# Pooled attention and an affine residual MLP on one core: the first mix freed of later row sums, batch 1's q over TensorE, and batch 1's attention placed later

## The chip, the cores and the metric

The kernel runs on one core of a Trainium2 chip. The metric is device time in microseconds (us), the median of several executions. Before the change it is 346.08 us (three runs, 345.53 to 347.93). The profile shown here is of one execution whose instructions span 343.4 us.

The engines are called TensorE (PE in the profile, with its weight loads as PEld), VectorE (DVE), ScalarE (ACT), GpSimd (POOL) and the sync engine (SP), which only issues transfers. "POOLq" and "SPq" are the instruction queues of GpSimd and the sync engine as issuers of transfers.

## The reference

There are 8 batches, 8 heads, 576 rows and a head width of 64, so a row over all heads is 512 wide. k and v are averaged over groups of 8 rows, which leaves 72 keys per head. Then follows a token mix over the 576 rows and a channel MLP of width 2048.

```python
k_p = k.reshape(B, H, Sp, pool, D).mean(axis=3)
v_p = v.reshape(B, H, Sp, pool, D).mean(axis=3)
scores = scale * np.matmul(q, k_p.transpose(0, 1, 3, 2))
attn = softmax(scores)                       # max subtracted, sum + 1e-9
x = heads_joined(np.matmul(attn, v_p))       # (B, 576, 512)

a1 = alpha1 * x + beta1
tok = np.einsum('ts,bsd->btd', w_tok, a1)
u = x + lam * tok
a2 = alpha2 * u + beta2
ch = np.maximum(a2 @ w_ch1, 0.0) @ w_ch2
out = u + lam * ch
```

## The kernel before

**Chunks and blocks.** The output rows are cut into chunks of 128 rows: four chunks `(b, 0)` to `(b, 3)` for each batch, and one chunk `(b, 4)` for each pair of batches that holds the last 64 rows of both. Four chunks make a block of the MLP, so there are nine blocks. Block 0 holds batch 0's four chunks, block 1 batch 1's four chunks.

**The MLP of a block.** `mlp_A(n, j)` (L641) computes one of 16 tiles of the hidden layer: four matmuls of 512 columns into `ps_h`, then a Relu on ScalarE into `Hj` (L658). `mlp_B(n, m, part)` (L663) computes a quarter of one output chunk: four matmuls of 512 columns into `ps_ch`. After part 3 VectorE multiplies by lam and adds u (L693, L694), and the sync engine stores the chunk.

**The attention of a batch.** It runs one batch ahead of its block: while TensorE works on block n, the attention of batch n + 1 is threaded in.

- `att_F` (L383) transposes q, either on TensorE with a ScalarE copy (L397, L404) or with a transposing transfer on the sync queue (L392). `att_K` (L432) pools k on TensorE after GpSimd has summed it (`sum_k`, L179). `att_S4` (L501) computes the scores of four heads, with the exponentials on ScalarE (L541); batch 0 uses `att_S` (L485) head by head.
- `sum_v` (L129) and `first_V` (L459) pool v for batch 1; later batches use `att_V` on VectorE (L476). Batch 1's v comes over `load_v32` (L117), on the GpSimd queue.
- `att_AV` (L545) multiplies the weights of one head with v: five matmuls of 66 columns (L556, L560), then a reciprocal and a product on VectorE (L562, L564) that write the head into `x_tm`. `att_X` (L574) makes `xs`, two heads at a time, on VectorE or GpSimd (L578, L571).

**Token mix.** `mix_T(b, c)` (L603) multiplies the transposed w_tok with all of `xs` of a batch: five matmuls of 512 columns into `ps_tok`. It therefore needs all eight heads of the batch. VectorE adds x (L614) and makes `u_bf` (L617), and `mix_uT` (L619) transposes that into `u_fm`, the MLP's input: in block 0 on TensorE with a copy on ScalarE (L631, L633), later with a transposing transfer on the sync queue (L626).

**Setup.** `setup_wtok(t)` (L318) transposes a block of w_tok on TensorE, and ScalarE copies it into `wtT`. `setup_rowsum(t)` (L331) computes the row sums of that block, which go into one more row of `wtT` and carry the beta term; `mix_T(0, c)` reads the row sums of block c. `setup_vectors` (L311) turns beta2 into columns. `keep_warm` (L597) issues matmuls whose result nobody reads. `load_w1(g)` and `load_w2(g)` (L357, L363) fetch parts of the two channel weights over the GpSimd queue; `load_w1(2)` is the last quarter of w_ch1.

**What sets the order.** The kernel schedules by hand. Up to block 0's first tiles the calls stand in the source in the order in which each engine gets them (L703 to L787). After that, each block makes a list `todo` of pairs of a position and a call (L841 to L877), sorted by position and issued in that order; one unit of position is one `mlp_A` tile or one `mlp_B` quarter. `mlp_A` of tile j stands at j, and `mlp_B` at 16 and later. Every engine runs its own instructions in that order, so a position ties an instruction only to its neighbours on its engine. Batch 1 has positions of its own (`first`), and the loads of batch 2 stand behind small memsets on VectorE (`gate`, `behind`) that hold them back.

The softmax here doesn't subtract the row's maximum and nothing guards it: scores larger than these inputs give would overflow.

## Time and profile before

| What | Value |
|---|---|
| Time, median of 3 runs | 346.08 us (345.53 to 347.93) |
| Span of the profiled execution | 343.4 us |
| First `mlp_A` of block 0 starts | 27.40 us |
| First mix of batch 1 starts | 54.44 us |
| First `mlp_A` of block 1 starts | 68.69 us |
| HBM read / written | 38.30 MB / 9.44 MB |
| Share of the chain of waits on TensorE | 83% |

The page gives for each engine its busy time, its share of the span and its number of instructions; then the span in 40 slices, each digit the busy share in tenths. `PEclk` is the clock that TensorE was granted, in the same tenths. A table of stretches lists, for each stretch of the span, the length and then the busy time of PE, PEld, DVE, ACT and POOL with instruction counts, then the clock, the DMA share and the rate in GB/s. A timeline line gives the start and the length in us, the engine, the line of the kernel, what is written and read with the shapes, and a count; in square brackets stands how long the engine was idle before it and what ended that. Neighbouring matmuls of one line are merged, and the length of a merged line reaches over into the next, since matmuls are pipelined; starts are the better guide.

### The profile page before, as it was taken

To read this page: it belongs to the slowest core of one execution; us is meant where nothing else is said; L and a number is where in the kernel's file an instruction comes from. 1 tells how busy PE (TensorE), PEld (TensorE's weight loads), DVE (VectorE), ACT (ScalarE), POOL (GpSimd) and SP (SyncE) were. 2 spreads that over 40 slices of the span, in tenths; PEclk is the share of its full clock that TensorE was granted. 3 is DMA by queue.
4 is the path that set the end of the run, shared out by engine and by line. 5 is a ranking of instruction groups with operands and counts; after the bars stand their busy time and mean duration, and the time that the engine had idled before them with its cause. 6 is when DMAs were issued, how large, how long until landed. Compare 5 with 4: busy or idle time off the path is not lost.

```text
span 343.4 us, 5828 instructions
## 1 busy us (share of the span) xinstructions
PE 333.8 (97%) x2162; PEld 176.4 (51%) x2198; DVE 222.1 (65%) x478; ACT 145.9 (42%) x275; POOL 91.1 (27%) x106
## 2 busy tenths in 40 slices
PE   7998999999999999999999999999999999999995
PEld 2767654455445544455445544554455445545544
DVE  6774388985777677866866697768675881037511
ACT  3756870069106820385038500880089006604700
POOL 8869507301153012701170218002600200000000
PEclk9999999999999999999999999999999999999999
DMA  8999999758688906794599439972910132011012
GB/s 119 201 212 329 200 210 275 156 139 140 159 231 162 176 1 175 165 226 58 159 173 208 67 111 216 170 125 67 239 42 1 48 76 76 2 61 62 2 51 71
DMA packets 67086, 46.03 MB, mean 134 GB/s; under 512 B 35401, under 2 KB 57293, under 8 KB 67058
## 3 DMA queue, kind: packets, MB, share of 16 engines
q1 hardware_dynamic: 52772, 32.99, 40.5%
q0 software_dynamic: 13824, 12.40, 21.7%
q8 instruction: 17, 0.28, 0.4%
q10 hardware_dynamic: 462, 0.27, 0.3%
q14 instruction: 11, 0.09, 0.1%
HBM read 38.30 MB, written 9.44 MB: 139 GB/s over the span
## 4 chain that ended last, share of the span: by engine, by line
PE 83%; DMA 9%; DVE 3%; POOL 1%; issue 1%; SPq 0%; ACT 0%; DVEq 0%; POOLq 0%
PE ps_ch L687 32%; PE ps_h L652 32%; PE ps_tok L610 11%; DMA w<-in_moe_w_ch_dram 4%; DMA rem_raw<-in_k_dram 2%; PE ps_av L556 2%; PE ps_s L512 2%; DMA q_bf<-in_q_dram 2%; DMA u_fm<-u_bf 1%; PE ps_ch L676 1%; DVE x_tm L564 1%; PE ps_kp L440 1%; PE ps_sc L492 1%; PE ps_r L519 1%; POOL k_raw L183 0%
## 5 line engine op out<-in xcount | busy, mean ns | idle before, releaser
L658 ACT ACTIVATE Hj<-ps_h,bias_cols 128x512 bf16<-128x512 f32 x144 | 97.9, 687 | 166.4 <-PE ps_h L652 163.9
L652 PE MATMUL ps_h<-u_fm,w 128*128 128x512 bf16 (+2 forms) x575 | 132.2, 374 | 2.1 <-ACT u_fm L633 0.7
L687 PE MATMUL ps_ch<-w,Hj 128*128 128x512 bf16 x543 | 128.5, 379 | 0.9 <-issue 0.5
L652 PEld LDWEIGHTS <-w 128*128 128x128 bf16 x592 | 64.1, 114 | 53.1 <-issue 3.9
L687 PEld LDWEIGHTS <-Hj 128*128 128x128 bf16 x560 | 52.9, 98 | 61.7 <-issue 1.6
L610 PE MATMUL ps_tok<-xs,wtT 128*128 128x512 bf16 (+2 forms) x199 | 44.7, 380 | 0.7 <-DVE xs L578 0.3
L693 DVE TENSOR_TENSOR ps_ch<-lam_bc,ps_ch 128x512 f32<-128x512 f32 x32 | 22.2, 693 | 34.0 <-PE ps_ch L687 33.8
L578 POOL TENSOR_TENSOR xs<-x_tm,lamal_bc 128x512 bf16<-128x512 f32 x10 | 12.6, 1268 | 110.2 <-DVE x_tm L564 110.2
L614 DVE TENSOR_TENSOR u_sb<-x_tm,ps_tok 128x512 f32<-128x512 f32 (+1 forms) x40 | 27.4, 684 | 11.9 <-PE ps_tok L610 11.9
L564 DVE TENSOR_TENSOR x_tm<-ps_av,rec 128x320 f32<-128x320 f32 x64 | 31.5, 492 | 2.7
L562 DVE RECIPROCAL rec<-ps_av 128x5 f32<-128x5 f32 x64 | 12.3, 193 | 31.7 <-PE ps_av L560 31.6
L694 DVE TENSOR_TENSOR u_sb<-u_sb,ps_ch 128x512 f32<-128x512 f32 x35 | 24.0, 687 | 13.6 <-PE ps_ch L687 12.5
L541 ACT ACTIVATE ET<-ps_s 72x512 f16<-72x512 f32 x56 | 32.3, 591 | 0.0
L610 PEld LDWEIGHTS <-wtT 128*128 128x128 bf16 (+3 forms) x200 | 17.4, 100 | 21.6 <-issue 2.5
L617 DVE TENSOR_TENSOR u_bf<-u_sb,al_bc 128x512 bf16<-128x512 f32 x34 | 25.6, 754 | 2.6 <-DMA u_fm<-u_bf 1.5
L480 DVE TENSOR_TENSOR v_u<-v_u 72x512 f32<-72x512 f32 (+1 forms) x48 | 26.4, 550 | 0.8
L183 POOL TENSOR_TENSOR k_raw<-k_raw 128x512 f32<-128x512 f32 x14 | 19.7, 1404 | 10.7 <-DMA k_raw<-in_k_dram 10.7
L556 PEld LDWEIGHTS <-ET 72*128 72x128 f16 x256 | 14.0, 97 | 9.1 <-DVE vp L473 0.4
L185 POOL TENSOR_TENSOR k_bf<-k_raw 128x512 bf16<-128x512 f32 x14 | 17.8, 1271 | 1.1
L79 POOL DMA_DIRECT2D q_bf<-in_q_dram x16 | 12.5, 784 | 15.3 <-DVE v_u L158 14.5
L578 DVE TENSOR_TENSOR xs<-x_tm,lamal_bc 128x512 bf16<-128x512 f32 x22 | 15.5, 705 | 0.7
L556 PE MATMUL ps_av<-vp,ET 72*128 72x66 f16 x256 | 15.6, 193 | 0.1
(130 smaller groups left out, 214.4 us busy)
## 6 DMA issues: line engine op xcount, KB each, us to landing
out_dram<-u_sb SPq DMA_DIRECT2D x32, 256.0 KB
k_raw<-in_k_dram SPq DMA_DIRECT2D x12, 512.0 KB
v_u<-in_v_dram SPq DMA_DIRECT2D x12, 512.0 KB
q_bf<-in_q_dram POOLq DMA_DIRECT2D x16, 256.0 KB, 6.2
w<-in_moe_w_ch_dram POOLq DMA_DIRECT2D x6, 512.0 KB, 15.3
w<-in_moe_w_ch_dram POOLq DMA_DIRECT2D x1, 1024.0 KB, 14.6
k_raw<-in_k_dram POOLq DMA_DIRECT2D x2, 512.0 KB, 16.8
v_main<-in_v_dram POOLq DMA_DIRECT2D x1, 1024.0 KB, 11.8
```

The source lines that it names most:

```text
L480: nc.vector.tensor_tensor(out=t[:, :, 0:n], in0=t[:, :, 0:n], in1=t[:, :, n:2 * n], op=ALU.add)
L541: nc.scalar.activation(out=o, in_=i, func=AF.Exp, bias=0.0, scale=0.125)
L556: nc.tensor.matmul(out=av[:, odd + c, :], lhsT=ET[:, m0:m0 + 128], rhs=vp1[:, hh, :])
L564: nc.vector.tensor_tensor(out=x[:, 1 - odd:6 - odd, dd:dd + D], in0=av[:, :, 0:64], in1=rec.unsqueeze(2).to_broadcast((P, 5, D)), op=ALU.mult)
L578: eng.tensor_tensor(out=xs[:, 0:4, cols], in0=x[:, 1:5, cols], in1=lamal_bc[:, cols].unsqueeze(1).to_broadcast((P, 4, D * (h1 - h0))), op= ...
L610: nc.tensor.matmul(out=ps_tok[p0:p1], lhsT=wtT[0:kk, at, P * c:P * c + p1 - p0], rhs=xs_pool[i][0:kk, sc, :], start=(sc == 0), stop=(sc == 4))
L614: nc.vector.tensor_tensor(out=s["u"][p0:p1, :], in0=x[p0:p1, 1 + c if c < 4 else 5 - 5 * i, :], in1=ps_tok[p0:p1, 0:DM], op=ALU.add)
L617: eng.tensor_tensor(out=s["u_bf"], in0=s["u"], in1=al2_bc, op=ALU.mult)
L652: nc.tensor.matmul(out=ps_h[:, t0:t1 + one], lhsT=w1_of(cc, j), rhs=rhs, start=(cc == 0), stop=(cc == 3))
L658: nc.scalar.activation(out=t, in_=ps_h, func=AF.Relu, bias=bias_cols[:, j:j + 1], scale=1.0)
L687: nc.tensor.matmul(out=ps, lhsT=Hj[n, j][:, 128 * m:128 * m + 128], rhs=w2[j // 4][:, j % 4, :], start=(j == 0), stop=(j == NJ - 1))
L694: nc.vector.tensor_tensor(out=u, in0=u, in1=ps, op=ALU.add)
```

## The change

Four things are changed; the computation is the same.

1. **Order of the prologue.** Head 4's `att_AV` moves ahead of head 6's scores. The w_tok transposes start earlier, and `mix_T(0, 0)` comes right after the row sums of block 1 instead of after those of block 2 and the fourth w_tok transpose. `setup_vectors` moves behind `mix_T(0, 1)`, with its second copy on ScalarE instead of VectorE. `mix_T(0, 3)` comes after the first two `mix_uT` instead of between them. There is one `keep_warm` matmul less. The aim is that the first mix waits only for what it reads.
2. **q of batch 1.** Its second half too is transposed on TensorE, at positions 2.6, 3.5, 4.4 and 5.3, instead of by a transposing transfer.
3. **Loads.** `load_w1(2)` is issued ahead of `load_v32(1)` instead of behind it.
4. **Batch 1's attention.** The row sums of v, `first_V` and the eight `att_AV` are placed later and closer together, the mixes start at 22.6 with a spacing of 1.2 instead of at 21.0 with 1.3, and the gated loads of batch 2 move from 14.5 to 17.5. This follows from the later v.

```diff
     def setup_vectors():
         ...
-        nc.vector.tensor_copy(out=u_fm[0][:, :, 0, 256], in_=ps[:, 0:4])
+        nc.scalar.copy(out=u_fm[0][:, :, 0, 256], in_=ps[:, 0:4])
...
-        if b > 1 or b == 1 and u:
+        if b > 1:
             if r == 0:
                 nc.sync.dma_start_transpose(out=st["qT"][u],
...
     att_S(0, 5)
+    att_AV(0, 4)
     att_S(0, 6)
-    att_AV(0, 4)
     spread_al1(1)
     att_AV(0, 5)
     att_X(0, 4, 6, nc.gpsimd, False)
     att_S(0, 7)
-    keep_warm(1)
+    setup_wtok(0, nc.scalar.copy)
     att_AV(0, 6)
-    setup_vectors()
     load_rem(1, behind=nc.vector)
     keep_warm(1)
-    setup_wtok(0, nc.scalar.copy)
+    setup_wtok(1, nc.scalar.copy)
+    keep_warm(1)
     att_AV(0, 7)
-    setup_wtok(1, nc.scalar.copy)
-    keep_warm(2)
+    keep_warm(1)
+    setup_rowsum(0)
     setup_wtok(2, nc.scalar.copy)
-    setup_rowsum(0)
     rest_X(0, 4, 6, nc.gpsimd)
     load_w1(1)
     keep_warm(1)
     setup_rowsum(1)
+    att_X(0, 6, 8)
+    mix_T(0, 0, nc.gpsimd)
     setup_rowsum(2)
     setup_wtok(3, nc.scalar.copy)
-    att_X(0, 6, 8)
-    mix_T(0, 0, nc.gpsimd)
-    load_v32(1)
+    load_w1(2)
     mix_T(0, 1)
+    setup_vectors()
     setup_rowsum(3)
     mix_T(0, 2, nc.gpsimd)
-    load_w1(2)
+    load_v32(1)
+    mix_uT((0, 0))
+    mix_uT((0, 1))
+    mix_T(0, 3)
     load_w2(0)
-    mix_uT((0, 0))
-    mix_T(0, 3)
-    mix_uT((0, 1))
     load_w2(1)
-    att_F(1, 2)
     mlp_A(0, 0, 0, 256)
...
         if first:
-            for hp in range(2):
-                todo.append((2.6 + 1.4 * hp, lambda hp=hp: att_F(b, hp)))
+            for hp in range(4):
+                todo.append((2.6 + 0.9 * hp, lambda hp=hp: att_F(b, hp)))
...
-            early = (5.7, 6.2, 4.2, 4.7) if first else (5.7, 6.2, 2.9, 3.4)
-            for i, dt in enumerate((2.9, 3.4, 4.6, 5.1) if u else early):
+            late = ((7.5, 8.1, 6.3, 6.9), (4.2, 4.8, 5.5, 6.1))[u]
+            for i, dt in enumerate(late if first else (2.9, 3.4, 4.6, 5.1) if u else (5.7, 6.2, 2.9, 3.4)):
                 h = 4 * u + i
                 todo.append((at + dt, lambda h=h: att_AV(b, h)))
...
             for i, u in enumerate((0, 2, 1)):
-                todo.append((10.4 + 0.1 * i, lambda u=u: sum_v(b, u)))
+                todo.append((12.7 + 0.1 * i, lambda u=u: sum_v(b, u)))
             for u in range(2):
-                todo.append((12.1 + 1.3 * u, lambda u=u: first_V(b, u)))
+                todo.append((14.6 + 0.9 * u, lambda u=u: first_V(b, u)))
...
         for c in range(5):
-            at = 21.0 + 1.3 * c
+            at = (22.6 + 1.2 * c) if first else 21.0 + 1.3 * c
...
-                    at = (14.51 if b == 1 else 21.0) + 0.01 * u
+                    at = (17.51 if b == 1 else 21.0) + 0.01 * u
                     todo.append((at, lambda b=b, u=u: load_k(b + 1, u, gate)))
...
-                    at = 14.55 + 0.01 * u if b == 1 else (6.7 if b == 2 else 3.5) + 4.0 * u
+                    at = 17.55 + 0.01 * u if b == 1 else (6.7 if b == 2 else 3.5) + 4.0 * u
                     todo.append((at, lambda b=b, u=u: load_v(
...
-                todo.append((14.5 if b == 1 else 20.9, lambda b=b: load_rem(b + 1, behind=gate)))
+                todo.append((17.5 if b == 1 else 20.9, lambda b=b: load_rem(b + 1, behind=gate)))
```

## The prediction

> **What bounds the kernel now.** I read four views, in this order: the page's busy rows and slices, the table of stretches, the timeline of each engine from 15 to 75 us, and the chain of waits in the same stretch.
>
> ```profile
> PE 333.8 (97%) x2162; PEld 176.4 (51%) x2198; DVE 222.1 (65%) x478; ACT 145.9 (42%) x275; POOL 91.1 (27%) x106
> PEclk9999999999999999999999999999999999999999
> 25.00:30.00 5.00, 4.09 (x38) 3.18 (x37) 3.16 (x9) 2.34 (x4) 4.98 (x8) 1.00 1.17 316
> 30.00:50.00 20.00, 19.94 (x204) 12.93 (x205) 9.76 (x31) 16.86 (x36) 8.58 (x9) 1.00 1.14 231
> 50.00:55.00 5.00, 4.69 (x36) 2.24 (x34) 4.51 (x12) 0.00 (x0) 2.46 (x3) 1.00 1.17 265
> 55.00:69.00 14.00, 13.90 (x69) 6.17 (x69) 12.29 (x18) 0.00 (x0) 6.28 (x6) 1.00 0.88 192
> ```
>
> After the stretch and its length come PE, weight loads, DVE, ACT, POOL, the clock, and DMA. TensorE is idle 343.4 - 333.8 = 9.6 us in all. Only two holes lie where the diff reaches: 0.91 us in 25 to 30 and 0.31 us in 50 to 55. From 30 to 50 TensorE has no hole to give back, and from batch 2 on the instruction orders of both kernels are the same. So the end moves by whatever the start of block 1 (68.69 us) moves.
>
> The two holes, and what runs into the second, in the timelines of TensorE and VectorE (start, length, instruction, count, idle before it):
>
> ```profile
> 27.40 0.60 PE L652 MATMUL ps_h<-u_fm,w 128*128 128x257 bf16 x4 [0.67 <-ACT u_fm L633]
> 30.00 1.93 PE L652 MATMUL ps_h<-u_fm,w 128*128 128x256 bf16 x16 [0.23 <-DVE bias_cols L655]
> 54.44 1.24 PE L610 MATMUL ps_tok<-xs,wtT 128*128 128x512 bf16 x5 [0.31 <-DVE xs L578]
> ...
> 44.89 0.20 DVE L562 RECIPROCAL rec<-ps_av 128x5 f32<-128x5 f32 x1 [0.53 <-PE ps_av L560]
> 51.61 0.18 DVE L562 RECIPROCAL rec<-ps_av 128x5 f32<-128x5 f32 x1
> 52.23 0.18 DVE L562 RECIPROCAL rec<-ps_av 128x5 f32<-128x5 f32 x1
> 53.60 0.69 DVE L578 TENSOR_TENSOR xs<-x_tm,lamal_bc 128x512 bf16<-128x512 f32 x1
> ```
>
> VectorE starts batch 1's eight heads at 44.89 us and works with only about 0.2 us of gaps until the last xs at 54.29, which starts mix_T(1,0) at 54.44. That run of VectorE work is the figure to carry along.
>
> Last, the sync queue ahead of block 1 (transposes of batch 1's u), and two u_bf products on VectorE:
>
> ```profile
> 64.84 1.19 SPq L416 DMA_TRANSPOSE rem_qT<-rem_q  x1
> 66.12 1.22 SPq L626 DMA_TRANSPOSE u_fm<-u_bf  x1
> 68.26 0.34 SPq L696 DMA_DIRECT2D out_dram<-u_sb  x1
> ...
> 59.10 1.31 DVE L617 TENSOR_TENSOR u_bf<-u_sb,al_bc 128x512 bf16<-128x512 f32 x1
> 64.07 0.69 DVE L617 TENSOR_TENSOR u_bf<-u_sb,al_bc 128x512 bf16<-128x512 f32 x1
> ```
>
> The last transpose that block 1 needs was issued at 66.12 and block 1 ran at 68.69: 2.57 us, with only 0.2 us of weight-load wait on it. So u_fm is already only just in time.
>
> **What the Trainium skill says.** "TensorE: Matmul & The Clock Gate", "Back-to-back issue gap": 518 cycles for 512 columns; the trace agrees, 0.86 us for four. Its "Part 1: The HAM clock gate" says the clock falls after an idle window of about 3.4 us; no hole in this trace is that long, the clock stays full in every slice, and my holes below stay under it. "SBUF — State Buffer", "SBUF: two separate sides": a VectorE operation with two SBUF inputs and a GpSimd operation that reads SBUF exclude each other. The trace agrees: L617 took 1.31 us at 59.10, while GpSimd summed k, against 0.69 us at 64.07.
>
> **Part by part.**
>
> *Prologue order.* The first mix now needs only rowsums 0 and 1 ahead of it; rowsum 2 and the fourth w_tok block follow. VectorE's last xs (19.92 to 20.9 us) is hardly moved: the removed bias copy (0.17 us) is offset by head 7's matmuls, which now stand behind one more w_tok transpose group. So mix_T(0,0) starts when that xs is there, at about 20.8 instead of 21.50. Behind it: rowsum 2 and w_tok 3 (0.28 each), mix 1 (1.08), the vector transpose (about 0.15), rowsum 3 (0.28), mix 2 (1.08), two groups of transposes (0.22 each), mix 3 (1.08). That puts the first mlp_A at 26.5 instead of 27.40, with its 0.67 us hole filled by mix 3. The next gate is u_bf of the fourth chunk (0.69 + 0.8 us on VectorE after mix 3), its transpose and ScalarE's 0.59 us copy: the second halves start at about 29.3 instead of 30.00. Gain 0.7 us; 0.55 if that gate binds fully, 0.88 if not. One filler matmul less (0.22) is inside this.
>
> *q over TensorE.* Eight more transposes (two groups of four, 0.22 us each by the group at 31.77): +0.44 us on the full engine. ScalarE's two more copies (0.59 each) lie in gaps of 0.3 to 0.7 us that it has from 30 to 48. The removed sync-queue transpose (27.61, 1.35 us) was awaited by nobody on the path.
>
> *Loads.* Before, v_main was issued at 24.78 and landed 11.8 us later (36.6); w_ch1's last quarter was issued at 27.55 and landed about 14.4 us later, at 42, just as setup_bias(3) wanted it (0.2 us of wait). Swapped, the weights come early and v last of the two, at about 42. Three row sums (0.67 + 0.42, 0.67, 0.67 + 0.42 = 2.85 us) then end at 45, against first_V(1,0) at 45.9: hidden, 1 to 2 us spare. w_ch2's third and fourth quarters landed about 15.7 and 15.0 us after 33.51 and 36.68; their issues move by about 0.4 us, and uses at about 51.9 and 53.6 leave over 1 us.
>
> *Batch 1's attention later.* Now the decisive sum. The first head goes from position 13.2 to 15.3, the last from 18.7 to 19.7, so eight heads are packed into 4.4 positions. Net of the prologue and the q transposes TensorE ends the first head's matmuls at about 47.1 us. From there to mix_T(1,0), now at 22.6 and behind part 3 of the first output chunk, it has first_V 0.22, seven heads at 0.15 and seven groups of four matmuls at 0.864: 7.3 us, so it arrives at 54.4. VectorE has, for the same stretch, eight heads at 0.63 (51.61 to 52.23), copies of vp 0.48, two xs pairs at 1.03 (0.69 + 0.29 and gaps), the gate memsets 0.5, the last xs 0.70, and about 0.4 for the longer first head and latencies: 9.1 us. It ends at about 56.3. TensorE waits about 2.0 us (1.5 to 2.3) where it waited 0.31: +1.7 us. One group of output matmuls has moved ahead of the wait, but it is in the 7.3 us and comes off later, so it changes nothing in the difference.
>
> *Start of block 1.* After mix_T(1,0) starts at 56.35, TensorE has 14.25 - 0.86 = 13.4 us (54.44 to 68.69 less that group): ready at 69.7. The transpose of the fourth chunk may not be: mix_T(1,3) is later (26.2), and its transpose (28.0) now stands on the sync queue behind the store of chunk m=2 (27), which waits for VectorE. VectorE's order after the last xs is m=0, u0, m=1, u1, u2, u3, m=2, each pair about 1.4 us: u_bf 3 ends at 65.6 to 66.2, m=2 at 67.0 to 67.6, store 0.35, transpose issued at 67.5 to 68.0, landing 2.57 us later at 70.0 to 70.6. That is 0.3 to 0.9 us of new wait; I take 0.5. The gates for batch 2's loads move from 48.05 to about 52.4; k and v then come some 4 us later, but k was ready at 62.9 for a use at 73.0, and v is next used at 70.2, moving to about 72: hidden.
>
> Sum: -0.7 + 0.44 + 1.7 + 0.5 = +1.9 us. 346.08 + 1.9 = 348.0.
>
> **Rivals.** (a) VectorE's run does not bind: the packed heads are drained while TensorE is in its seven groups, and only the prologue's gain and the extra transposes remain, with the 0.31 us hole closed: -0.7 + 0.44 - 0.31 = -0.6, 345.5; at best 345.2. For it: TensorE is the busy engine, and the attention is moved by about as much as the mixes (2.1 and 1.6 positions). Against: VectorE took 9.4 us for this work without real gaps, and 7.3 us is all it is given. (b) The wait at the first mix comes, but u_fm is in time: -0.7 + 0.44 + 1.7 = +1.4, 347.5. (c) A load joins in: v lands at 45 rather than 42, holding first_V, all heads and VectorE by some 2 us, or the sync queue holds u_fm behind v loads of batch 2 by 2 to 3 us. Then +4 to +5, 350 to 351. For it: v is read from a queue whose transfers took 11.8 to 17.9 us; against: bytes and order ahead of it are those that ended at 42.
>
> **How the numbers follow.** Waits at both places, +1.6 to +2.6 us: 50 in 100. (b): 23. (a), wholly or in part: 17, nearly all of it within 1% of before. (c): 10. The likeliest gives 348.0. The range leaves out most of (c) and the tail of (a): 345.5 to 349.4. Over 1% slower means 349.5 or more: (c) and a little of the first, 0.11. Over 1% faster would need 3.5 us, and the holes in reach sum to 1.2: 0.02. The rest, 0.87, is within 1%.
>
> **What would show it.** In the changed profile: mix_T(0,0) at 20.8 and the first mlp_A at 26.5 without the 0.67 us hole; sixteen q transposes between 31 and 36 us; mix_T(1,0) with about 2 us of idle laid to VectorE's xs, near 56.3; block 1 at about 70.2 with a wait on u_fm; later blocks 36 us apart as before. Wrong if mix_T(1,0) starts without a wait, if the row sums of v wait for their load past 43 us, or if the clock leaves full speed.

## The result: 350.05 us, slower by about 1%

| | Before | After |
|---|---|---|
| Time, median (range), 4 runs each beside each other | 346.06 us (345.53 to 347.93) | 350.05 us (349.49 to 351.48) |
| Ratio, with its 95% interval | | 1.0112 (1.0063 to 1.016) |
| Span of the profiled execution | 343.4 us | 348.2 us |
| First mix of batch 1, idle ahead of it | 54.44 us, 0.31 us | 58.81 us, 1.97 us |
| First `mlp_A` of block 1, wait on u_fm | 68.69 us, none | 73.48 us, 1.11 us |

Predicted were 348.0 us and 345.5 to 349.4, so the kernel lost twice what was foreseen. Executions over 1.5% above the fastest of their kernel are counted as slow; the ratios and the clock counts below leave them out, the medians do not. From block 1 to the end both kernels take the same 274.7 us (343.4 - 68.69 and 348.2 - 73.48): the loss lies ahead of block 1, as argued.

**One yardstick first.** The two profiles are already apart where nothing was changed. The first line is of the timeline of TensorE before, the second of that after: the same two matmuls of `spread_al1(0)`.

```profile
9.40 0.69 PE L308 MATMUL ps_bc<-vecs,ones_row 1*128 1x256 f32 x2
```

```profile
9.32 1.22 PE L308 MATMUL ps_bc<-vecs,ones_row 1*128 1x256 f32 x2
```

In the second profile TensorE still ran at half pace until about 13.8 us, in the first it was at full pace from about 9. The clock column shows 1.00 in both, but the traces hold no record of the clock before 14.19 and 8.80 us. The two matmuls of `first_V(0, 1)` on L469 are the last instructions ahead of the first reordered call; they began at 15.35 and 16.82 us, and in all 20 profiles of this document, with the same instructions up to there, anywhere from 14.95 to 19.03. So 4 us of spread come in before the change begins, and medians of 4 to 22 executions carry some of it. I therefore give starts as **us after that pair** (marked +). Block 1 began at +53.34 before (68.69 - 15.35) and at +56.66 after (73.48 - 16.82): **3.32 us** is what the change cost in the profile.

The stretches after, with the columns of the prediction's table:

```profile
55.00:60.00 5.00, 2.97 (x14) 1.25 (x14) 4.57 (x15) 0.00 (x0) 3.09 (x4) 1.00 0.33 85
70.00:75.00 5.00, 3.89 (x18) 1.70 (x17) 4.15 (x8) 0.43 (x1) 0.00 (x0) 1.00 1.10 249
```

TensorE has two new holes, around 58 and 73 us, while VectorE is busy for 4.57 and 4.15 of 5 us. TensorE's timeline names what ended them:

```profile
22.31 1.25 PE L610 MATMUL ps_tok<-xs,wtT 128*128 128x512 bf16 x5 [0.33 <-DVE xs L578]
...
28.21 0.60 PE L652 MATMUL ps_h<-u_fm,w 128*128 128x257 bf16 x4
...
31.14 1.92 PE L652 MATMUL ps_h<-u_fm,w 128*128 128x256 bf16 x16 [0.23 <-DVE bias_cols L655]
...
46.51 0.27 PE L512 MATMUL ps_s<-qT,kp 64*72 64x256 bf16 x1 [0.22 <-ACT ET L541]
...
58.81 1.24 PE L610 MATMUL ps_tok<-xs,wtT 128*128 128x512 bf16 x5 [1.97 <-DVE xs L578]
...
73.48 4.51 PE L652 MATMUL ps_h<-u_fm,w 128*128 128x512 bf16 x20 [1.11 <-DMA u_fm<-u_bf]
```

The 0.67 us hole at the first `mlp_A` is gone, as intended. The 1.97 us are VectorE's: its timeline shows the run from the first head to the last xs, 49.53 to 58.66. Then come the u_bf products. Those of chunks 1 to 3 took 1.13, 1.05 and 0.86 us, against 0.69 undisturbed; the last is shown.

```profile
49.53 0.20 DVE L562 RECIPROCAL rec<-ps_av 128x5 f32<-128x5 f32 x1 [0.54 <-PE ps_av L560]
...
57.97 0.69 DVE L578 TENSOR_TENSOR xs<-x_tm,lamal_bc 128x512 bf16<-128x512 f32 x1
...
67.50 0.86 DVE L617 TENSOR_TENSOR u_bf<-u_sb,al_bc 128x512 bf16<-128x512 f32 x1
```

And the sync queue ahead of block 1: the last transpose, whose u_bf was done at 68.36, stands behind the store of the third chunk and is issued at 70.13. It lands 3.3 us later; before, block 1 began 2.57 us after the issue of that transpose, without a wait.

```profile
67.88 1.58 SPq L626 DMA_TRANSPOSE u_fm<-u_bf  x1
69.71 0.37 SPq L696 DMA_DIRECT2D out_dram<-u_sb  x1
70.13 1.21 SPq L626 DMA_TRANSPOSE u_fm<-u_bf  x1
```

### The profile page after: what moved, and what is told of

Read it like the earlier page. It is cut to its first block, busy times and chain, and to the rows that moved or that the text cites. A ratio compares the mean times of both kernels' runs of the same rounds, so it can differ in the third digit from the quotient of the medians.

```text
span 348.2 us, 5840 instructions
## 1 busy us (share of the span) xinstructions
PE 336.6 (97%) x2169; PEld 177.5 (51%) x2205; DVE 223.1 (64%) x477; ACT 146.9 (42%) x278; POOL 91.1 (26%) x106
## 4 chain that ended last, share of the span: by engine, by line
PE 88%; DVE 5%; DMA 3%; issue 2%; ACT 1%; POOL 0%; SPq 0%; DVEq 0%; ACTq 0%
PE ps_h L652 35%; PE ps_ch L687 29%; PE ps_tok L610 10%; DMA u_fm<-u_bf 3%; PE ps_s L512 2%; PE ps_av L556 2%; DVE x_tm L564 1%; PE ps_warm L601 1%; PE ps_ch L676 1%; PE ps_sc L492 1%; PE ps_kp L440 1%; DVE u_sb L614 1%; PE ps_q L397 1%; DVE xs L578 1%; DVE ps_ch L693 1%
## 5 line engine op out<-in xcount | busy, mean ns | idle before, releaser
L578 POOL TENSOR_TENSOR xs<-x_tm,lamal_bc 128x512 bf16<-128x512 f32 x10 | 12.6, 1267 | 113.6 <-DVE x_tm L564 113.6
L694 DVE TENSOR_TENSOR u_sb<-u_sb,ps_ch 128x512 f32<-128x512 f32 x35 | 24.0, 687 | 13.6 <-PE ps_ch L687 12.5
L617 DVE TENSOR_TENSOR u_bf<-u_sb,al_bc 128x512 bf16<-128x512 f32 x34 | 26.5, 779 | 2.2 <-DMA u_fm<-u_bf 1.1
L183 POOL TENSOR_TENSOR k_raw<-k_raw 128x512 f32<-128x512 f32 x14 | 18.8, 1344 | 10.9 <-DMA k_raw<-in_k_dram 10.9
L79 POOL DMA_DIRECT2D q_bf<-in_q_dram x16 | 12.6, 794 | 15.2 <-DVE v_u L158 14.4
```

The source lines that it names most:

```text
L578: eng.tensor_tensor(out=xs[:, 0:4, cols], in0=x[:, 1:5, cols], in1=lamal_bc[:, cols].unsqueeze(1).to_broadcast((P, 4, D * (h1 - h0))), op= ...
L617: eng.tensor_tensor(out=s["u_bf"], in0=s["u"], in1=al2_bc, op=ALU.mult)
```

## The experiments

Profiles are read at the yardstick. "Clock" counts the executions whose mean granted clock was lowered (at most 0.995, against 0.998 to 1.0 in the rest). Each kernel ran beside the kernel before, whose medians were 346.7 to 347.1 us.

| Kernel | First mix of batch 1 (idle) | Block 1 (wait on u_fm) | Median us | Ratio to before | Clock |
|---|---|---|---|---|---|
| before | +39.09 (0.31) | +53.34 (0) | | | 3 of 206 |
| e5 changed kernel again | +42.01 (1.97) | +57.40 (0.16) | 349.78 | 1.0091 (1.0050 to 1.0132) | 6 of 10 |
| e1 without part 4 | +39.22 (0.31) | +53.47 (0) | 347.24 | 1.0010 (0.9981 to 1.0040) | 0 of 14 |
| e2 part 4 alone | +43.28 (1.97) | +57.88 (1.05) | 349.69 | 1.0087 (1.0057 to 1.0116) | 4 of 16 |
| e3 transpose ahead of store | +42.01 (1.97) | +55.77 (0.21) | 349.64 | 1.0077 (1.0049 to 1.0105) | 4 of 13 |
| e7 shorter VectorE run | +40.86 (0.86) | +55.82 (1.41) | 348.60 | 1.0065 (1.0038 to 1.0091) | 3 of 17 |
| e9 fillers in the hole | +41.98 (0.25) | +56.58 (1.04) | 351.66 | 1.0137 (1.0082 to 1.0192) | 0 of 6 |
| e10 parts 1 and 3 alone | +40.61 (0.24) | +54.91 (0) | 348.28 | 1.0034 (1.0009 to 1.0059) | 6 of 19 |
| e11 mixes later still | +41.99 (0.25) | +56.14 (2.33) | 349.98 | 1.0109 (1.0057 to 1.0161) | 1 of 6 |
| e8 heads early, mixes late | +39.62 (0) | +55.14 (1.97) | 349.69 | 1.0101 (1.0049 to 1.0154) | 2 of 6 |
| e12 e3 and e7 together | +40.89 (0.85) | +55.14 (0.70) | 349.36 | 1.0061 (1.0032 to 1.0090) | 1 of 20 |
| e13 second scores later | +42.20 (1.96) | +56.88 (1.13) | 349.36, one run | | 0 of 1 |
| e14 fillers, and e3 | +42.00 (0.24) | +56.60 (1.05) | 348.52 | 1.0052 (1.0015 to 1.0089) | 0 of 14 |
| e15 e8 and e3 | +39.63 (0) | +54.33 (1.14) | 348.07 | 1.0038 (1.0007 to 1.0069) | 3 of 21 |
| e16 e15, q by transfer | +39.21 (0) | +53.78 (1.01, put down to VectorE) | 350.32 | 1.0044 (1.0009 to 1.0079) | 2 of 13 |
| e17 e15, gates early | +39.62 (0) | +53.01 (0) | 346.67 | 1.0013 (0.9989 to 1.0036) | 2 of 22 |
| e18 changed, gates early | +41.40 (1.38) | +54.99 (0) | 349.41 | 1.0060 (1.0029 to 1.0091) | 2 of 22 |
| e19 e17, q by transfer | +43.56 (0) | +56.95 (0) | 349.78 | 1.0034 (0.9989 to 1.0079) | 3 of 8 |
| e20 part 2 alone | +39.49 (0.30) | +53.75 (0) | 347.76 | 1.0016 (0.9984 to 1.0048) | 0 of 14 |

### Which part costs the time: e5, e1, e2

The changed kernel once more; the changed kernel with part 4 undone; the kernel before with part 4 alone. For e1 (e2 does the reverse to the kernel before):

```diff
-            at = (22.6 + 1.2 * c) if first else 21.0 + 1.3 * c
+            at = 21.0 + 1.3 * c
-                todo.append((12.7 + 0.1 * i, lambda u=u: sum_v(b, u)))
+                todo.append((10.4 + 0.1 * i, lambda u=u: sum_v(b, u)))
... first_V, heads and gates in the same way
```

> The changed kernel once more, unaltered, for its time in more rounds and for a second look at its first 17 us. The two profiles at hand differ by 1.47 us already at the instruction before the first changed one (second first_V of batch 0: 15.35 us before, 16.82 us after), because TensorE kept its slow matmuls (0.61 us for a 256-column fp32 matmul instead of about 0.31) until about 13.8 us instead of about 9 us. Theory A (the loss is the change's own, 3.3 us after that point: 0.4 prologue and scores, 2.0 and 1.1 us of new waits): the ratio stays near 1.010, +3.3 us, and the start of the slow stretch varies from run to run for both kernels. Rival B (the slow first 15 us belong to the changed kernel): the ratio stays at +4 to +5 us and the second profile again has its first_V at about 16.8 us.

> The changed kernel with part 4 alone undone: row sums of v, first_V, heads, mixes and gates of batch 1 back at their old positions; prologue order, q over TensorE and the load order stay. Theory A: VectorE gets its old run time before the mix, so the mix's wait falls from 1.97 us to 0.3 or less and the u_fm wait from 1.11 us to under 0.3: about 346.3 us, +0.0 to +0.6 against before. Rival C (the loss comes from parts 1 to 3, for instance v landing late or ScalarE's extra q copies): it stays at +2 us or more.

> The kernel before with part 4 alone: heads, mixes and gates of batch 1 at the new positions, everything else as before. Theory A: the same waits as in the changed kernel, about 2 us at the first mix of batch 1 and 0.6 to 1.1 us at block 1, so +2.3 to +3.0 us. Rival C: within 0.5 us of before, since v and q are as early as before.

e5 began its pair at 15.32 us, so the slow first 14 us of the first profile do not belong to the change. e1 is the kernel before within 0.3%, and e2 loses what the changed kernel loses: **part 4 is the whole loss**, and parts 1 to 3 together bring nothing measurable. e2's block 1 is 1.2 us later still, for one wait of 1.20 us at 43.06 us for w_ch1's last quarter (`setup_bias(3)`, L378), which with the old load order stands behind v. In the changed kernel, with the weights ahead of v, that wait is gone.

### The hole at the mix: e7, e11, e13

e7 takes 1 us of work out of VectorE's run; e11 places the mixes two groups later; e13 moves the second score group behind one more tile.

```diff
e7
-                    eng = nc.gpsimd if h == 5 else nc.vector
+                    eng = nc.gpsimd if h == 5 or first and h == 1 else nc.vector
e11
-            at = (22.6 + 1.2 * c) if first else 21.0 + 1.3 * c
+            at = (24.55 + 0.75 * c) if first else 21.0 + 1.3 * c
-                todo.append((at + 1.8, lambda key=key: mix_uT(key)))
+                todo.append((at + (0.15 if first else 1.8), lambda key=key: mix_uT(key)))
e13
-            at = (9.0 if first else 6.3, 13.6)[u]
+            at = (9.0 if first else 6.3, 14.2 if first else 13.6)[u]
... the four heads of u = 1 keep their places
```

> The changed kernel, but the xs pair of batch 1's heads 0 and 1 (0.69 + 0.29 us on VectorE) is made on GpSimd. Theory A (VectorE's run from the first head to the last xs sets when the first mix of batch 1 can start): the run is 1.0 us shorter, the mix's idle time falls from 1.97 to about 1.0 us, block 1 starts about 1 us earlier, and the time falls from about 349.9 to about 348.7; if the 1.97 us hole is what lowers the clock, the granted clock stays at 1.0 as well and the time is nearer 348.0. Rival (the mix waits for something else, for instance the exponentials or v): the hole stays at about 2.0 us and the time at 349.8.

> The changed kernel, with batch 1's mixes two groups of output matmuls later (24.55 instead of 22.6, spacing 0.75 instead of 1.2) and each transposing transfer issued 0.15 behind its mix, ahead of the store of the third chunk. Theory A (two groups of 0.864 us fill the hole of 1.97 us with work that is due anyway): the idle time ahead of the mix falls to about 0.2 to 0.3 us, the clock stays at 1.00, block 1 starts 2 to 3 us earlier than in the changed kernel unless the last transpose comes late, and the time is 346.5 to 347.5. Rival (VectorE is the bound of this whole stretch, so that the wait only moves from the first mix to block 1's input): the wait on u_fm at the start of block 1 grows by as much as the hole at the mix shrinks, and the time stays within 0.5 us of 349.8.

> The changed kernel with the second score group of batch 1 at 14.2 instead of 13.6, one mlp_A tile later, its heads unmoved. Theory A (that group waits 0.22 us for the exponentials of the first, and this wait delays the first head and so VectorE's run): the wait is gone, VectorE's first reciprocal comes 32.5 us after the second ps_v pair of the prologue instead of 32.7, and the mix starts 0.2 to 0.3 us earlier; the exponentials of the second group are not late. Rival (nothing follows from it, as ScalarE then brings the second group's exponentials later): the mix starts at 42.0 us as before or later.

e7: the run is 1 us shorter, and the mix starts 1.13 us earlier. VectorE sets that moment. e11 shows the same from the other side: with two groups of work put into the hole the mix still starts at +41.99, as in the changed kernel. Its timeline of TensorE:

```profile
60.37 1.24 PE L610 MATMUL ps_tok<-xs,wtT 128*128 128x512 bf16 x5 [0.25 <-DVE xs L578]
...
74.52 6.17 PE L652 MATMUL ps_h<-u_fm,w 128*128 128x512 bf16 x20 [2.33 <-DMA u_fm<-u_bf]
```

The first hole is filled and the second has grown from 1.11 to 2.33 us: the rival was right, the wait only moved. Work ahead of a late start does not help if what the late start feeds is waited for as well.

e13's 0.22 us wait is gone, but in its profile TensorE also waited 0.59 us in the prologue for an exponential, so its starts have to be taken from the second halves of block 0's tiles: the mix begins 27.15 us after these, against 27.67 in the changed kernel. On TensorE the second score group took 1.20 us in the changed kernel (46.00 to 47.20), 0.72 in e13 and 0.89 before. So it lost 0.5 us against e13, and 0.3 us against the kernel before. This rests on one profile of each.

### The wait on u_fm: e3, e12, e8, e15, e17, e18

```diff
e3 (the last u transpose ahead of the third chunk's store)
-                todo.append((at + 1.8, lambda key=key: mix_uT(key)))
+                todo.append((at + (0.75 if first and c == 3 else 1.8), lambda key=key: mix_uT(key)))
e8 (row sums, first_V and heads back, mixes and gates as changed)
-                todo.append((12.7 + 0.1 * i, lambda u=u: sum_v(b, u)))
+                todo.append((10.4 + 0.1 * i, lambda u=u: sum_v(b, u)))
... first_V and the heads in the same way
e17 (e8 with e3) and e18 (the changed kernel), gates of batch 2's loads back
-                    at = (17.51 if b == 1 else 21.0) + 0.01 * u
+                    at = (14.51 if b == 1 else 21.0) + 0.01 * u
... load_v 17.55 to 14.55 and load_rem 17.5 to 14.5
```

> The changed kernel with one call moved: the transpose of batch 1's fourth chunk is issued at position 26.95 instead of 28.0, so that on the sync queue it stands ahead of the store of chunk m=2. Theory A: the store waited for VectorE's two products (68.28 to 69.69) and held the transpose until 70.13 although its u_bf was ready at 68.36; now it is issued at about 69.5 after the third transpose and lands 3.3 us later, so the u_fm wait falls from 1.11 us to about 0.4 and the time by 0.5 to 0.8 us. Rival D (the transposes are late because of the traffic of batch 2's late loads, not the queue): the wait stays at 1 us and the time is the same.

> The changed kernel with two edits that were run alone before: the xs of heads 0 and 1 of batch 1 on GpSimd, and the last u transpose ahead of the third chunk's store. Theory A (VectorE's run delays the mix, and the order on the sync queue delays the transpose; the two add up): block 1 starts 54.6 to 54.9 us after the second ps_v pair of the prologue (56.7 in the changed kernel, 55.8 with either edit alone), with the 0.9 us hole at the mix left and a wait on u_fm of at most 0.3; the time is about 348. Rival (VectorE's backlog takes back what the sync queue gains): 55.5 or more.

e3 takes 0.9 us off block 1's start, but its later blocks took 275.5 us instead of 274.7, and little of it is seen in the time. In e12 the two reliefs do not quite add up (+55.14; 54.6 to 54.9 was expected). The fourth u_bf was done at the same moment in e3, e12 and e14, 9.47 to 9.48 us after the first mix, and in all three its transpose stands ahead of the store; yet the wait was 0.21, 0.70 and 1.05 us. So the store is a part of the wait, not its cause.

> The changed kernel, with batch 1's row sums of v, first_V and eight heads put back to the old positions; its mixes (22.6, spacing 1.2) and the gates of batch 2's loads (17.5) stay where the change put them. Theory A (the later heads are the loss, since they make VectorE's run of 9.1 us end after TensorE has come to the mix): VectorE's run starts about 3 us earlier, TensorE has two groups of output matmuls more ahead of the mix, so the hole at the mix vanishes, block 1 starts 53.2 to 53.6 us after the second ps_v pair of the prologue (53.3 before, 56.7 in the changed kernel) without a wait on u_fm, and the time is that of before within 0.3%. Rival (the later mixes and transposes are what makes block 1 late): no hole at the mix, but a wait on u_fm of 1 us or more at block 1, and 347.5 to 348.5 us.

> The changed kernel with the heads, first_V and row sums of batch 1 at the old positions, the mixes late as in the changed kernel, and the last u transpose ahead of the third chunk's store. The same kernel without that last edit had no hole at the mix but a wait of 1.97 us on u_fm at block 1, which began 55.1 us after the second ps_v pair of the prologue (53.3 in the kernel before). Theory A (there the transpose stands behind a store that waits for VectorE; issued as soon as its u_bf is there, it lands in time): the transpose is issued about 1.8 us earlier, the wait on u_fm falls to 0.2 to 0.4 us, block 1 begins at 53.2 to 53.6, and the time is that of before within 0.3%. Rival (the mixes are simply too late for block 1, whatever the queue does, since mix, two products, transfer and landing take about 7 us): a wait of 1.0 us or more stays, 54.2 or later, and a time 0.3 to 0.6% over before.

I was wrong about e8: with VectorE's run early the hole at the mix vanished, and a wait of 1.97 us on u_fm stood in its place. With the transpose freed of the store (e15) 1.14 us of it stayed. The rival was right as to the number, but its reason ("the mixes are simply too late") wasn't the whole, as e17 shows. The timelines of VectorE and of GpSimd in e15:

```profile
63.83 1.77 DVE L617 TENSOR_TENSOR u_bf<-u_sb,al_bc 128x512 bf16<-128x512 f32 x1
```

```profile
63.79 1.27 POOL L185 TENSOR_TENSOR k_bf<-k_raw 128x512 bf16<-128x512 f32 x1
```

The fourth u_bf began 0.04 us after GpSimd's sum of batch 2's k and took 1.77 us: 1.08 us more than the 0.69 it takes alone, almost the whole 1.27 of GpSimd's operation. It is the exclusion that the prediction cited from the Trainium skill ("SBUF — State Buffer", "SBUF: two separate sides"), and here the measurement agrees again. I took this for the cause of the wait, and e17 was made to test it. But the product is not what block 1 waited for. It was done at 65.60. The sync queue, with the third and fourth transposes in one line:

```profile
64.53 3.39 SPq L626 DMA_TRANSPOSE u_fm<-u_bf  x2
```

The third of them took 2.08 us of this and held the queue until 66.61, 1 us after the product was done; only then could the fourth be issued.

So it is the **transposing transfers** that came late. What slows them lies with the **gates**, which e15 and the changed kernel have at 17.5 instead of 14.5. At the yardstick the first load of batch 2's k is issued 3.8 us later in e15 than in e17, which has the gates back, and 5.3 us later in the changed kernel than before; v's loads follow it. They are then still moving when block 1's last transposes are issued.

> As the kernel with early heads, late mixes and the transpose ahead of the store (block 1 at 54.33 us after the second ps_v pair, wait on u_fm 1.14), with the gates of batch 2's loads back at 14.5 instead of 17.5. There VectorE's fourth u_bf product took 1.77 us instead of 0.69, while GpSimd summed batch 2's k from 58.94 to 65.06. Theory A (the later gates move GpSimd's sums of k onto the u_bf products that block 1 waits for, and the two engines shut each other out): the k sums start 2 us or more earlier, the fourth u_bf takes 0.69 to 0.9 us, the wait falls to 0.1 to 0.3 us and block 1 begins at 53.2 to 53.5 us; the time is that of before within 0.3%. Rival (the length of that product has another cause, or the k loads come no earlier since they queue behind others): 1.77 us as before, a wait of 1 us, 54.2 or later.

> The changed kernel with only the gates of batch 2's loads back at 14.5. Theory A (the later gates slow three u_bf products by 0.44, 0.36 and 0.17 us and so make about 0.9 of the 1.11 us of wait on u_fm): the hole at the mix stays at 1.9 to 2.0 us, the u_bf products take 0.69 to 0.75 us, the wait at block 1 falls to 0.1 to 0.5 us and block 1 begins at 55.7 to 56.1 us after the second ps_v pair instead of 56.7; the time falls by about 0.7. Rival (VectorE's memsets or the k sums now fall on the heads and xs of batch 1 and lengthen VectorE's run): the mix comes later than 42.0 us by as much, and block 1 at 56.5 or later.

With the gates back, e17's block 1 starts at +53.01 without any wait, 0.33 us ahead of before. Its third transpose held the queue for 1.22 us, and the two together took 0.86 us less than in e15:

```profile
64.36 2.53 SPq L626 DMA_TRANSPOSE u_fm<-u_bf  x2
```

The expectation named the wrong cause, though: GpSimd's sums began only 0.6 us earlier than in e15, not 2, and the fourth product still took 1.05 us. e18 sizes the gates in the changed kernel. Its timelines of TensorE and of the sync queue:

```profile
59.66 1.24 PE L610 MATMUL ps_tok<-xs,wtT 128*128 128x512 bf16 x5 [1.38 <-DVE xs L578]
...
73.25 4.51 PE L652 MATMUL ps_h<-u_fm,w 128*128 128x512 bf16 x20
```

```profile
68.53 1.22 SPq L626 DMA_TRANSPOSE u_fm<-u_bf  x1
...
70.78 1.20 SPq L626 DMA_TRANSPOSE u_fm<-u_bf  x1
```

One edit, the gates, takes 1.67 us off block 1's start (+56.66 to +54.99), half of the 3.32. The hole at the mix shrinks by 0.59, since the gates' memsets (0.5 us) left VectorE's run. The wait on u_fm of 1.11 us goes, and again hardly through the products: two of the four still took 0.94 and 0.93 us, the fourth was done 9.38 us after the first mix instead of 9.55, and the last transpose was issued 0.20 us sooner after the mix. The rest is the transfer. Block 1 began 2.47 us after the last transpose was issued, without a wait; in the changed kernel it was 3.35 us with one. Stretches at the third transpose, of the changed kernel and then of e18 (the last two columns are DMA share and GB/s):

```profile
68.00:70.00 2.00, 1.95 (x13) 0.82 (x11) 1.97 (x4) 0.00 (x0) 0.00 (x0) 1.00 1.40 237
```

```profile
69.00:70.00 1.00, 0.98 (x9) 0.33 (x5) 0.97 (x3) 0.00 (x0) 0.00 (x0) 1.00 0.24 46
```

Rival D of e3's expectation, the traffic of batch 2's late loads, was thus right in the main. In the changed kernel packets of v's loads and of two stores ran until 69.8 us; in e18, whose loads of k were issued 9.6 us sooner after the pair, those of v's loads were over at 60.9. No experiment separates the loads of k from those of v, or slows the transfers without moving the gates. In time e18 gained only some 0.3% on e5, less than its profile; the medians' spread hides the rest.

### The clock after a hole: e9, e14

In e5's profile the granted clock halved just after the hole that ended at 57.33 us. These are its stretches of 1 us (the last but two columns give the clock):

```profile
57.00:58.00 1.00, 0.68 (x3) 0.35 (x4) 0.94 (x3) 0.00 (x0) 0.94 (x3) 0.88 0.60 100
58.00:59.00 1.00, 1.00 (x3) 0.29 (x2) 0.97 (x2) 0.00 (x0) 0.63 (x1) 0.50 0.79 272
...
61.00:62.00 1.00, 1.00 (x5) 0.40 (x4) 0.93 (x2) 0.00 (x0) 0.92 (x2) 0.91 0.71 235
```

e9 and e14 put eight matmuls on zeros into that hole, e14 on top of e3.

```diff
+            todo.append((22.55, lambda: fill(8)))
+    def fill(count):
+        ps = gp("ps_fill")
+        for _ in range(count):
+            nc.tensor.matmul(out=ps, lhsT=warm[:, 0:P], rhs=warm)
```

> The changed kernel, with eight matmuls of 512 columns on zeros (0.216 us each, 1.73 us in all), whose result nobody reads, just ahead of batch 1's first mix: they lie in the hole of 1.97 us. Theory A (the hole lowers the clock afterwards in many runs, and that is a part of the loss of about 3.4 us): the mix starts at the same moment after VectorE's xs, the clock then stays at 1.00 in the profile, and the time falls from about 349.9 by 0.5 to 1.6 us, to 348.3 to 349.4. Rival (the lowered clock seen after the hole was chance and has nothing to do with it): 349.8 or up to 0.2 more, for the fillers that overrun.

> The changed kernel with the eight fillers of zeros in the hole ahead of batch 1's first mix, and the last u transpose ahead of the third chunk's store, so that neither hole of more than 1 us is left on TensorE. Theory A (such holes let the granted clock fall in many runs): with the same instructions otherwise the mean clock stays at 0.998 or more in all runs but one in ten, against about one in three with the holes unfilled (store edit alone), and the fastest third of the times is unchanged at about 348.2. Rival (the falls come from the short waits of the prologue or by chance): a mean clock of 0.996 or less in a quarter of the runs or more.

TensorE's timeline in e9: the mix starts no earlier (+41.98), but TensorE is busy meanwhile.

```profile
54.79 1.89 PE L606 MATMUL ps_fill<-warm 128*128 128x512 bf16 x8
```

With the hole filled no execution in 20 (e9, e14) had a lowered mean clock; with the hole of 1.97 us open ahead of the mix 17 of 43 had it (3 of 4 of the first runs of the changed kernel, 6 of 10 in e5, 4 of 13 in e3, 4 of 16 in e2). e2, e3 and e5 ran on one chip, e9 and e14 on two others, but the kernel before, beside them, differed little: 1 of 38, none of 34, and 2 of 33. So the hole very likely does it. The time that I expected back in e9 was not seen: 351.66 us, the median of only six executions and above the changed kernel's, while its profile spans 346.5 us. Why is open; a lowered clock is not the reason. e14, with 15, was 348.52. What a fall costs is thus not well measured. In e5's profile it was 0.74 us (block 1 at +57.40 instead of +56.66), as part of it ran into the wait on u_fm. e14's name promised too much: a wait of 1.05 us on u_fm stayed, and did not lower the clock.

### q over TensorE: e10, e16, e19, e20

```diff
e10, e16, e19 (second half of batch 1's q by transfer, as before); e20 the reverse, in the kernel before
-        if b > 1:
+        if b > 1 or b == 1 and u:
             if r == 0:
                 nc.sync.dma_start_transpose(out=st["qT"][u],
...
+    att_F(1, 2)
```

> The kernel before with part 1 (order of the prologue) and part 3 (order of the loads) of the change only; batch 1's second q half goes by the sync queue and its attention stands at the old positions. Theory A (part 1 gains 0.3 to 0.7 us, part 2 costs 0.44, part 4 is the whole loss): 0.3 to 0.7 us under before, and about 0.4 under the kernel that lacks only part 4 (which was 347.24 beside 346.71), so 346.1 to 346.6 on the same scale. Rival (q over TensorE is hidden and parts 1 and 3 bring nothing): no difference from before, and none from the kernel that lacks only part 4.

> As the kernel with early heads, late mixes and the transpose ahead of the store, and the second half of batch 1's q by the sync queue as in the kernel before. Theory A (q over TensorE costs 0.44 us on the full engine; parts 1 and 3 gain 0.28 us on the block's start; the late mix gives back the hole of 0.31 us): block 1 begins 52.7 to 53.1 us after the second ps_v pair, 0.4 us ahead of the kernel with q over TensorE, and the time is 0.0 to 0.2% under before. Rival (q's transposes are hidden, or the sync queue's transfer of q delays something): no difference between the two, or a later block 1.

> As the first of this call, with the second half of batch 1's q by the sync queue (as before the change). Theory A (all waits that part 4 makes are gone and the q term of 0.42 us too): block 1 begins 52.7 to 53.1 us after the second ps_v pair, 0.2 to 0.6 us ahead of before (53.34), and the time is 0.1% under before, within its uncertainty. Rival (something in this order still holds block 1's input): 53.4 or later.

> The kernel before with part 2 of the change only: the second half of batch 1's q is transposed on TensorE, and the transposing transfer of it (issued near 27.6 us) is gone. Theory A (that transfer slows the big loads beside it: with it v took 11.8, 12.6, 13.7, 12.5 and 17.2 us from issue to landing, without it 7.8 to 11.5): v lands at most 10.5 us after its issue, and the four w_ch parts issued from 22 to 35 us take a median of at most 13.5 us instead of 15.9; block 1 begins 53.3 to 53.8 us after the second ps_v pair (53.34 before), 0.42 more for the transposes, less what a wait for w_ch1 gave. Rival (the later place of v in the queue set its landing in those kernels, not the transfer): v lands after 11.3 us or more, and the w_ch parts after 15 us or more.

The eight transposes cost 0.41 us in e20 (+53.75 against +53.34); e16, whose wait on u_fm was about as long as e15's, is 0.55 ahead of it, 0.42 already at the first mix. e10, which was to show the same, can't: its prologue waited 0.53 us for w_tok and its clock fell, and block 1 began 1.57 us later than before. The price of 0.44 was right, and it is not hidden. But the transfer is not free either. e19, meant as the best version (+52.7 to +53.1 expected, +56.95 found), has it back, and its VectorE waited for v:

```profile
46.29 0.69 DVE L137 TENSOR_TENSOR v_main<-v_main 128x512 f32<-128x512 f32 x1 [4.01 <-DMA v_main<-in_v_dram]
```

TensorE then stood idle for 2.55 us ahead of `first_V`. From issue to landing v had taken 17.2 us in e19, 13.7 in e10 and 12.5 in e16. The fourteen profiled kernels that also have v behind the weights, but q over TensorE, show 7.8 to 12.6 us, the less the later the yardstick pair began (e20's expectation said 7.8 to 11.5, and left out e9). Like starts compared: 17.2 against 9.5 and 11.0 (pair at 17 us), 13.7 against 11.0 to 12.6 (at 15 us), 12.5 against 7.8 to 8.6 (from 18 us on). In e20 the transfer alone was removed from the kernel before. The loads issued from 22 to 35 us, of before and then of e20 (KB each, and the median us to landing):

```profile
w<-in_moe_w_ch_dram POOLq DMA_DIRECT2D x4, 512.0 KB, 15.9
v_main<-in_v_dram POOLq DMA_DIRECT2D x1, 1024.0 KB, 11.8
```

```profile
w<-in_moe_w_ch_dram POOLq DMA_DIRECT2D x4, 512.0 KB, 12.5
v_main<-in_v_dram POOLq DMA_DIRECT2D x1, 1024.0 KB, 10.9
```

The weights come 3.4 us sooner; v's 10.9 lies between the two expectations, and e20's pair began 1.7 us later than that of before, which by itself shortens such landings. So the transfer probably delays the loads beside it, and with v behind the weights (part 3) that can reach the heads; e19's 2.55 us is of one profile. The clock counts lean the same way: e10 and e19 have a lowered clock in 9 of 27 executions, and e1 and e17, the same order with q over TensorE, in 2 of 36; e16 and e15 don't differ (2 of 13, 3 of 21).

No version was measurably faster than the kernel before. e17, with the changed kernel's parts 1 to 3, is the nearest: 0.33 us ahead at block 1, and 1.0013 (0.9989 to 1.0036) in time.

## Why the prediction was right or wrong

**Right.** The end moved by what the start of block 1 moved. VectorE's run was 9.13 us (49.53 to 58.66; 9.1 predicted) and the hole ahead of the mix 1.97 us (2.0): the central step. q over TensorE cost 0.41 us (0.44). v landed at 39.9 us and w_ch1 in time, so the loads of part 3 were hidden. Rival (a), that VectorE's run does not bind, fell with the 1.97 us. Rival (c) has the right number, 350 to 351 us, by luck in the main: v did not come late. Its second half, u_fm held behind batch 2's v loads, is near to what happened, but they cost about 0.9 us and not 2 to 3.

**Wrong: "hidden" for batch 2's loads.** The step judged only whether k and v come in time for their use. They did. What it did not ask is what the late loads run beside: block 1's last transposes (only rival (c) comes near this). For these it took the landing from the kernel before, 2.57 us, where the DMA engines moved 96 GB/s in the 3 us from 64.8 us on. Every other term of the step held, counted from the first mix: the fourth u_bf done after 9.55 us (9.25 to 9.85 predicted), the third chunk's products after 10.88 (10.65 to 11.25), the transpose issued after 11.32 (11.15 to 11.65), TensorE ready after 13.56 (13.4). From that issue to block 1's start it was 3.35 us, 0.78 more. So the wait was 1.11 us instead of 0.5, beyond the 0.3 to 0.9 that it allowed. e18, with the loads early, has the landing back at 2.47 us or less and no wait. The exclusion of VectorE and GpSimd, cited two paragraphs earlier and not carried over, did slow three products. But by the chain of waits only the fourth lay on the path, and it took 0.17 us more than 0.69.

**Mis-sized: the prologue.** The first mix did start 0.66 us earlier at the yardstick (+5.49 against +6.15), and the first `mlp_A` hole was filled. But the second halves began at +14.32 instead of +14.65: 0.33 us, not 0.7. The gain must pass three gates, and the text itself named the last (u_bf of the fourth chunk); its bottom of 0.55 was still too high.

**Missing: the second score group.** With the first head and `first_V` now behind it, it came sooner after the first group and met that group's exponentials. It took 1.20 us instead of 0.89: 0.3 us.

**The sum.** With measured terms: -0.33 + 0.41 + 0.31 + 1.66 (1.97 - 0.31) + 1.11 = 3.16, against the 3.32 of the profiles; 0.16 us are not assigned. The prediction's own sum (+1.9) and its times (block 1 at 70.2, which is +1.5) did not agree by 0.4 us; comparing the two would have shown that TensorE's arrival at the mix was put too early. From the prediction's +1.9 to 3.32 the largest terms are the wait on u_fm (0.6), the prologue (0.4) and the score group (0.3).

**Wrong: "my holes below stay under it".** The clock was taken as safe because the Trainium skill ("TensorE: Matmul & The Clock Gate", "Part 1: The HAM clock gate") gives an idle window of about 3.4 us. Here holes of 1.97 us (e5), 2.33 us (e11) and 0.53 us (e10, ahead of 18.24 us, for w_tok) were each followed within 1.2 us by 3.4 us at 0.50, and the first runs of the changed kernel had a lowered clock in 3 of 4. The page's window length agrees with how long a fall lasts, not with how long a hole must be. The rest between the profile's 3.3 us and the measured medians (+3.1 and +4.0) can come from this and from the first 15 us; how much of each is open.

## What to carry to other kernels

When a load or its gate is moved, ask also what transfers it will run beside, and whether one of them is on the path; asking only whether it comes in time for its use is half the question. When an operation is found slowed, check that the next step was waiting for it before calling it the cause: e15's product lost 1.08 us that block 1 did not wait for. An engine's run of work that sets a start can't be beaten by placing other work ahead of that start: either the run begins earlier, gets shorter, or the wait moves on. And before two profiles of a short effect are compared, find the last instruction that the change can't have touched and measure from there.

## What the runs showed of the hardware

- TensorE's slow first stretch ended between about 8 and 19 us, where each trace's first record of the clock begins; until then only the durations tell (1.22 us instead of 0.69 for the pair on L308). The pair on L469 moved by 4 us.
- In the five profiles with a fall of the clock (e5, e8, e10, e11, e19) it lasted 3.4 us at 0.50 each time, worked out from the stretches of 1 us, and began 0.1 to 1.2 us after a hole had ended. A hole of the same length brings it in some executions only. With a hole of 1.97 us open ahead of the mix the mean clock was lowered in 17 of 43 executions; with the hole filled by matmuls on zeros, in none of 20.
- One transposing transfer of 128 x 512 took the sync queue 1.2 us in a quiet stretch and up to 2.6 us beside large loads (e16, at 67.45 us). By the semaphore records of the traces all four of block 1's landed 2.4 to 2.5 us after their issue in e18; in the changed kernel, beside batch 2's loads, the third took 4.3 us and the fourth 3.3.
- A VectorE product of 128 x 512 with two SBUF inputs, 0.69 us alone, took 1.77 us when it began 0.04 us after a GpSimd sum of 1.27 us (e15).
